# Loading x's third block second, x's rows in order of use, and block 3's spare rows from SyncE's queue

## The chip, the cores and the metric

The kernel runs on one core of a Trainium2 chip. The metric is the device time of one execution in microseconds, as the median of several runs. Besides these there is one execution with the hardware profiler on; all rows of a profile or a trace come from that one.

## What is computed

x has 2048 tokens of 448 features. The result mixes an attention branch and an MLP branch with one gate per token:

```python
x = A_x
g = _sigmoid((x * gate_w).sum(-1, keepdims=True))
a = _A_ref(x, A_wq, A_wk, A_wv, A_wo)       # 16 heads of 28, one shared key and value head
b = _B_ref(x, B_w1, B_w2, B_w3, B_w4)
return g * a + (1 - g) * b
```

The part that this change touches is the first half of the MLP branch:

```python
h = _gelu(_layernorm(x, axis=-1) @ w1)
# quarters of h's features are shifted by +1, -1, +2, -2 tokens: hs = concat(g0, g1, g2, g3) @ w2
x1 = x + hs
return x1 + _gelu(_layernorm(x1, axis=-1) @ w3) @ w4
```

## The kernel before, in words

The tokens are worked in four blocks of 512, numbered 0 to 3; a block has four tiles of 128 tokens. A float32 product is made of two or three products of rounded parts: an operand is split into a high and a low part (`split_x`, `split_w_chunk`, `h_part`), by a copy that rounds (ScalarE, mostly) and a subtraction (VectorE or GpSimd). The order of the instructions on each engine is that of the code.

The stages before the long MLP and attention loops, which is where the change is made:

- **Loads.** x comes in twice. `load_x(b)` (L284) brings block b transposed from `in_xT_dram` (1024 KB, tiles `xkv_b`), for the queries and for w1; `load_x1(b)` (L293) brings the same tokens as rows (896 KB, from `in_x_dram` into `x1`), for the layernorm's statistics and the residual. Nearly all loads are issued by SyncE (SP); a transfer of SyncE's queue is issued once the one before it has been, and once what it waits for has come.
- **Queries.** `first_queries` and `stage_q(u)` multiply the blocks of x by wq. `q_out(u)` (L327) copies a result out of PSUM on ScalarE and stores it to DRAM (`qd`), from ScalarE's queue but for u = 3 and the last, which SyncE stores.
- **Centring w1.** The layernorm's mean is taken out of w1 instead of out of x. `centre_w1` (L384) sums the columns of w1's transpose on VectorE (L388), writes the sums to DRAM in four small transfers (`cd`, L393) and reads them back to all partitions (`mean`, L395). `minus_mean` (L400) subtracts them on VectorE; then w1 is split (`split_w_high`, `split_w_low`: L113 to L116 on ScalarE, a memset of the upper half of its last chunk on GpSimd, L114, and L120 and L121 on VectorE).
- **w1 and gelu.** `stage_w1(b)` (L440) multiplies block b by w1 (L448 to L452), four tiles, each followed by a gelu on ScalarE (`hf`, L456), whose scale is the layernorm's 1/std (`rs_s`, from `ln1_tile`: L146 and L147 on VectorE, L150 and L151 on GpSimd), and a transpose on VectorE (`ht`, L457). The block is then written to DRAM by SyncE (`hd`, L462) and read back by `h_read(b)` (L467) in another layout, as `hraw`. There is one buffer of the tag `hraw`, so the next read waits until the block before has been split; xkv_3 uses it first.
- **Shift and w2.** `h_parts(b)` splits hraw into `hh` and `hl`, the operands of w2 (ScalarE L482, VectorE and GpSimd L483). hh and hl have 112 partitions of features and 16 spare ones, which `spare_h(b)` (L428) fills with the rest of the low part, by four small transfers inside the chip: from SyncE's queue for blocks 0 to 2, from ScalarE's for block 3. `stage_w2(b)` (L499) multiplies by w2 (L504, L505, L507) into one of two PSUM banks (`hs`), and VectorE adds a bank to x's rows (L509), which frees it.
- **Second layernorm, w3, w4.** Block 0 is normed, transposed through DRAM (`xd`, written at L174, read at L179 and L181 into `xr`) and split (`ln_split`, L673 and L676); `load_w34(i)` (L649, L650) loads the MLP's weights, which are split behind the tiles of the last w2 block (`weights`).

Buffers are taken from tags with a fixed number of them: `raw` has two (wqraw, xkv_0, then xkv_2, later ht and xt4), `hh` has two (w2raw, later hh of each block). All transfers share eight completion semaphores (DMAHW0 to DMAHW7 in the orders below), and an issue on a semaphore waits until the earlier transfer on it has landed.

Of the kernel before, what the change touches and what calls it, by code (L numbers as in the profile page):

```python
# [9 lines left out]
F32 = mybir.dt.float32  # L10
F32R = mybir.dt.float32r
# [6 lines left out]
P = 128  # L18
# [6 lines left out]
NB = S // 512  # L25
# [12 lines left out]
def f32(ap):  # L38
    return ap.bitcast(F32)
# [3 lines left out]
def gated_mix_kernel(  # L43
# [65 lines left out]
            nc.vector.tensor_tensor(wl[0:64, 3, :], raw[0:64, 3, :], f32(wh)[0:64, 3, :], ALU.subtract)  # L109
            nc.scalar.copy(wl[64:128, 3, :], raw[64:128, 3, :])  # L110

    def split_w_high(raw, wh, wl):
        nc.scalar.copy(wh[:, 0:3, :], raw[:, 0:3, :])  # L113
        nc.gpsimd.memset(f32(wh)[64:128, 3, :], 0.0)  # L114
        nc.scalar.copy(wh[0:64, 3, :], raw[0:64, 3, :])
        nc.scalar.copy(wl[64:128, 3, :], raw[64:128, 3, :])  # L116

# [147 lines left out]
    with tc.tile_pool(name="s1b", bufs=1) as s1b, \  # L265
# [10 lines left out]
        def h_tile(tag, name):  # L276
            return s1b.tile([P, 2112], F32R, tag=tag, bufs=2, name=name)[:, 0:2064].rearrange("p (m n) -> p m n", m=4)
# [6 lines left out]
        def load_x(b):  # L284
            if b == 1:
                xraw[b] = f32(s1b.tile([P, 4, 512], F32R, tag="w2x", bufs=1, name="xkv_1"))
            elif b == 3:
                xraw[b] = s1.tile([P, 4, 512], F32, tag="hraw", bufs=1, name="xkv_3")
            else:
                xraw[b] = s1.tile([P, 4, 512], F32, tag="raw", bufs=2, name=f"xkv_{b}")  # L290
            nc.sync.dma_start(xraw[b], xT[:, :, 512 * b:512 * b + 512])

        def load_x1(b):  # L293
            nc.sync.dma_start(x1[:, 4 * b:4 * b + 4, :],
                              x[512 * b:512 * b + 512, :].rearrange("(t p) d -> p t d", p=P))
# [11 lines left out]
        s1.tile([P, 16], F32, name="gap_w1")  # L307
        w1h = s1.tile([P, 4, D], F32R, name="w1h")
        w1l = s1.tile([P, 4, D], F32R, name="w1l")
        s1.tile([P, 48], F32, name="gap_x")  # L310
        w2h = s1b.tile([P, 4, D], F32R, name="w2h")
        w2l = s1b.tile([P, 4, D], F32R, name="w2l")
# [14 lines left out]
        def q_out(u, ps):  # L327
            b, g = divmod(u, NG)
            qf = s1.tile([P, 512], F32, tag="qf", bufs=4, name=f"qf_{u}")
            nc.scalar.copy(qf, ps)  # L330
            (nc.sync if u in (3, NU - 1) else nc.scalar).dma_start(qd[g, :, 512 * b:512 * b + 512], qf)

        def first_queries():
            ps = [mm1(f"q_{g}") for g in range(NG)]
# [49 lines left out]
        def centre_w1():  # L384
            cs = s1.tile([P, 32], F32, name="cs")
            nc.gpsimd.memset(cs, 0.0)
            for c in range(4):
                nc.vector.reduce_sum(cs[0:C, c:c + 1], w1t[0:C, c, :], axis=AX.X)  # L388
            ct = s1.tile([P, 32], F32, name="ct")
            nc.vector.transpose(ct, cs)  # L390
            cd = dram.tile([4, P], F32, name="cd")
            for p in range(4):
                nc.sync.dma_start(cd[:, 32 * p:32 * p + 32], ct[32 * p:32 * p + 4, :])  # L393
            mean = s1.tile([P, 4, P], F32, tag="hf", bufs=3, name="mean")
            nc.sync.dma_start(mean, cd.unsqueeze(0).broadcast_to([P, 4, P]))  # L395
            return mean[:, :, 0:C]

# [27 lines left out]
            o = min(c[0], 4 * 516 - 2 * step)  # L425
            return flat[:, o:o + 2 * step].rearrange("i (m n) -> i m n", m=2)[:, :, c[0] - o:c[0] - o + 512]

        def spare_h(b, queue):  # L428
            low = f32(hl[b])
            queue.dma_start(shifted(hh[b], 0, 2), low[0:32, 0, 1:513])  # L430
            queue.dma_start(shifted(hh[b], 2, 2), low[32:64, 0, 1:513])
            queue.dma_start(shifted(hl[b], 1, 2), low[64:96, 0, 1:513])
            queue.dma_start(shifted(hl[b], 3, 1), low[96:112, 0, 1:513])

        def low_w2(m):
            nc.vector.tensor_tensor(w2l[0:C, m, :], w2raw[0:C, m, :], f32(w2h)[0:C, m, :], ALU.subtract)
# [48 lines left out]
        def h_parts(b, m0, m1):  # L485
            if m0 == 0:
                h_begin(b)
            for m in range(m0, m1):
                h_part(b, m)
                if m == 0 and b < NB - 1:  # L490
                    spare_h(b, nc.sync)
            if m1 == 4:
                for tt in (hh, hl):
                    if b:
                        nc.gpsimd.tensor_copy(tt[b - 1][0:C, :, 514:516], f32(tt[b])[0:C, :, 2:4])
                    if b == NB - 1:
                        nc.gpsimd.memset(f32(tt[b])[0:C, :, 514:516], 0.0)
# [16 lines left out]
        s1b.tile([P, 16], F32, name="gap_hl")  # L514
        w1raw = f32(h_tile("hl", "w1raw"))[:, :, 0:D]
        w1t = f32(h_tile("hl", "w1t"))[:, :, 0:D]
        nc.sync.dma_start(w1t[0:C, :, :], w1T.rearrange("(q p) n -> p q n", p=C))
        nc.sync.dma_start(w1raw, w1)
        high_x(0, 1, 2)
# [4 lines left out]
        split_w_chunk(wqraw, wqh, wql, 3)  # L524
        split_w_chunk(wqraw, wqh, wql, 0)
        q0 = first_queries()
        load_x(2)
        split_x(1, 0, 2)
        split_x(1, 2, 4)
        for g in range(NG):  # L530
            q_out(g, q0[g])
        mean = centre_w1()
        load_x1(0)
        s1b.tile([P, 32], F32, name="gap_hh")
        w2raw = f32(h_tile("hh", "w2raw"))[:, :, 0:D]
        nc.sync.dma_start(w2raw[0:C, :, :], w2.rearrange("(q p) n -> p q n", p=C))
        s1b.tile([P, 16], F32, name="gap_w2")
        load_x(3)
        for b in range(1, NB):
            load_x1(b)  # L540
        split_x(2, 0, 2)
        split_x(2, 2, 4)
        split_x(0, 0, 1)
# [4 lines left out]
            ln1_tile(0, t)  # L548
        stage_q(6)
        stage_q(7)  # L550
        split_w_high(w1raw, w1h, w1l)
        split_w_low(w1raw, w1h, w1l)
        stage_q(8)
        for t in range(4):
# [124 lines left out]

        xraw2[0] = big("xr_0").rearrange("p (c n) -> p c n", c=4)  # L680
        xt_read(0, xraw2[0])
        spare_h(NB - 1, nc.scalar)
        load_w34(0, s2a)
        vT = s2a.tile([P, 512], F32, tag="xn", bufs=1, name="vT")
        nc.gpsimd.memset(vT, 0.0)
# [504 lines left out]
```

## Time and profile before

| What | Value |
|---|---|
| Median of 3 runs | 912.26 us (912.13 to 913.19) |
| The profiled execution | 913.44 us |
| its span, first to last instruction | 911.6 us |
| TensorE busy | 900.1 us of the span |
| ScalarE, VectorE, GpSimd busy | 629.2, 523.8, 72.0 us |
| TensorE's granted clock, mean | 0.997 |

The prediction quotes several views of this execution. The page has the busy times. The timeline gives instructions in order of time (start, duration, engine, line, operation, output<-input; in brackets the engine's idle time before it and what ended that). The chain of waits follows the work that ended last back from its end. A view of waits has engine, line, what was waited for, and us in all, times, longest. PE is TensorE, ACT ScalarE, DVE VectorE, POOL GpSimd, SPq SyncE's queue of issues; L456 is line 456 of the kernel. A `DMA` piece runs to the landing of the transfer.

### The profile page before, as it was taken

Reading aid. Unit: us, or ns where it says so; the run is one execution under the profiler, and the core shown is the slowest. Engines: PE = TensorE matmul, PEld = TensorE weight load, DVE = VectorE, ACT = ScalarE, POOL = GpSimd, SP = SyncE. Lnnn points to the kernel's source line nnn. Section 1 sums busy time; section 2 is a strip of 40 time slices with the busy share of each in tenths; the row PEclk is TensorE's granted clock in tenths of the full one; section 3 lists DMA queues with packets and bytes.
Section 4 is the critical chain, followed back from the end, with each engine's and each line's share of the span. In section 5 each row is a group of like instructions: output and inputs, shape, how many; then the busy total and the mean of one; then the engine's idle time right before and its main releaser. Section 6 shows DMA issues by size and latency. Waiting matters only on the chain.

```text
span 911.6 us, 24209 instructions
## 1 busy us (share of the span) xinstructions
PE 900.1 (99%) x10390; PEld 628.7 (69%) x10390; DVE 523.8 (57%) x978; ACT 629.2 (69%) x998; POOL 72.0 (8%) x109
## 2 busy tenths in 40 slices
PE   9998999999999999999999999999999999999997
PEld 6897888888888888875555555555555555555554
DVE  4484563831431531136766776776677766767664
ACT  4523254332131231269999999999999999999994
POOL 1022400510000520020000000000000000000000
PEclk9999999999999999999999999999999999999999
DMA  9867766030120020010000001000011000010001
GB/s 297 290 171 201 189 191 171 13 99 1 34 54 1 18 69 1 1 51 24 15 25 15 23 15 55 23 25 16 24 33 36 25 14 25 15 55 14 15 15 44
DMA packets 51146, 54.77 MB, mean 60 GB/s; under 512 B 11964, under 2 KB 38316, under 8 KB 50924
## 3 DMA queue, kind: packets, MB, share of 16 engines
q1 hardware_dynamic: 47980, 48.03, 18.5%
q10 hardware_dynamic: 3056, 5.16, 1.6%
q8 instruction: 82, 1.34, 0.6%
q14 instruction: 28, 0.23, 0.1%
HBM read 36.35 MB, written 15.33 MB: 57 GB/s over the span
## 4 chain that ended last, share of the span: by engine, by line
PE 86%; DMA 8%; DVE 2%; ACT 2%; SPq 0%; issue 0%; POOL 0%; ACTq 0%; DVEq 0%; POOLq 0%
PE bank L936 26%; PE bank L207 19%; PE bank L886 6%; PE acc L737 5%; PE acc L735 5%; PE acc L736 5%; PE g L139 4%; PE g L140 4%; PE g L138 4%; PE pair L207 3%; DMA xkv<-in_xT_dram 2%; DMA x<-in_x_dram 2%; PE g L141 1%; PE g L142 1%; DMA hd<-ht 1%; DMA hraw<-hd 1%
## 5 line engine op out<-in xcount | busy, mean ns | idle before, releaser
L260 ACT ACTIVATE p<-bank 128x512 f32<-128x512 f32 x514 | 266.3, 607 | 4.8 <-PE bank L207 1.5
L936 PE MATMUL bank<-p,vext 128*32 128x256 f32 x4064 | 247.6, 382 | 0.4
L936 PEld LDWEIGHTS bank<-p,vext 128*32 128x32 f32 x4064 | 117.6, 109 | 116.0 <-ACT p L260 52.8
L998 DVE COPY p<-pair 128x1024 f32<-128x1024 f32 x125 | 153.1, 1225 | 57.5 <-PE pair L207 45.0
L725 ACT ACTIVATE gh<-g 128x512 fp32r<-128x512 f32 x55 | 32.9, 598 | 181.1 <-PE g L142 181.1
L860 DVE TENSOR_TENSOR o<-o,bank 128x256 f32<-128x256 f32 x222 | 93.5, 421 | 80.3 <-PE bank L936 70.2
L260 ACT ACTIVATE p<-p 128x1024 f32<-128x1024 f32 x126 | 138.1, 1096 | 0.0
L260 ACT ACTIVATE p<-pair 128x1024 f32<-128x1024 f32 x129 | 136.7, 1059 | 0.0
L727 DVE TENSOR_TENSOR gl<-gf,gh 128x512 fp32r<-128x512 f32 x55 | 39.8, 725 | 161.4 <-ACT gf L726 161.4
L207 PE MATMUL bank<-qh,kh 32*128 32x512 f32 x514 | 114.7, 444 | 0.0
L207 PE MATMUL pair<-qh,kh 32*128 32x512 f32 x510 | 113.9, 443 | 0.0
L207 PE MATMUL bank<-qh,kl 32*128 32x512 f32 x514 | 101.6, 389 | 0.0
L207 PE MATMUL bank<-ql,kh 32*128 32x512 f32 x514 | 101.3, 390 | 0.0
L207 PE MATMUL pair<-qh,kl 32*128 32x512 f32 x510 | 101.0, 389 | 0.0
L207 PE MATMUL pair<-ql,kh 32*128 32x512 f32 x510 | 100.6, 389 | 0.0
L207 PEld LDWEIGHTS bank<-qh,kh 32*128 32x128 f32 x514 | 47.5, 181 | 60.3 <-issue 37.9
L737 PE MATMUL acc<-w4h,gl 128*128 128x448 f32 x220 | 80.7, 367 | 0.0
L735 PE MATMUL acc<-w4h,gh 128*128 128x448 f32 x220 | 80.1, 364 | 0.0
L736 PE MATMUL acc<-w4l,gh 128*128 128x448 f32 x220 | 79.8, 363 | 0.0
L886 PE MATMUL bank<-wof,on 128*32 128x224 f32 (+1 forms) x984 | 69.5, 357 | 0.0
L140 PE MATMUL g<-ah,w3l 128*128 128x512 f32 x168 | 65.4, 389 | 0.0
L138 PE MATMUL g<-ah,w3h 128*128 128x512 f32 x168 | 65.4, 389 | 0.0
(200 smaller groups left out, 1389.0 us busy)
## 6 DMA issues: line engine op xcount, KB each, us to landing
rb<-rd SPq DMA_DIRECT2D x15, 256.0 KB
qd<-qf ACTq DMA_DIRECT2D x14, 256.0 KB
x<-in_x_dram SPq DMA_DIRECT2D x4, 896.0 KB
hd<-ht SPq DMA_DIRECT2D x16, 224.0 KB
hraw<-hd SPq DMA_DIRECT2D x4, 896.0 KB
xd<-xt SPq DMA_DIRECT2D x16, 224.0 KB
w34raw<-in_w_dram SPq DMA_DIRECT2D x7, 512.0 KB
qr<-qd SPq DMA_DIRECT2D x64, 56.0 KB
```

The lines of the kernel that those rows point to most:

```text
L138: nc.tensor.matmul(ps, wh[:, c, :], ah[:, c, :], start=(c == 0), stop=False)
L140: nc.tensor.matmul(ps, wl[:, c, :], ah[:, c, :], start=False, stop=False)
L207: nc.tensor.matmul(ps[j], k[h, keys], q[h, :], start=(r == 0), stop=(r == 2), tile_position=(32 * j, 0))
L260: nc.scalar.activation(p[:, heads], p[:, heads] if source is None else source, AF.Exp, scale=SCALE)
L727: nc.vector.tensor_sub(gl, gf, f32(gh))
L735: nc.tensor.matmul(ps, gh[:, tok], w4h[i][:, k, :], start=(f == 0), stop=False)
L736: nc.tensor.matmul(ps, gh[:, tok], w4l[i][:, k, :], start=False, stop=False)
L737: nc.tensor.matmul(ps, gl[:, tok], w4h[i][:, k, :], start=False, stop=(f == stop))
L860: nc.vector.tensor_add(o, o, pv)
L886: nc.tensor.matmul(ps[32 * i:32 * i + 32, :], a[:, c:c + 32], w, start=start, stop=stop, tile_position=(0, 32 * i))
L936: nc.tensor.matmul(pv[32 * j:32 * j + 32, :], vext[:, kt, :], p_of[k][:, j, qs], start=(k == ks[0]), stop=(k == ks[-1]), tile_position=(0, ...
L998: nc.vector.tensor_copy(pa[:, both], pairs[0])
```

## The change

Five edits, all ahead of the long loops:

- xkv_2 is loaded right behind xkv_1, ahead of w1's transpose and w1. It takes a buffer of the tag `hh` (2112 elements a partition, of which it uses 2048) instead of one of `raw`, which came free only when wqraw had been split.
- Rows of x are loaded in the order of use: block 0 ahead of the mean's read-back, block 1 ahead of w2raw, block 2 ahead of xkv_3, block 3 behind it. Before, block 0 came behind the mean, and blocks 1 to 3 behind w2raw and xkv_3.
- Query 3's store goes from SyncE's queue to ScalarE's.
- The upper half of w1h's last chunk is set to zero where the tile is made, instead of where w1 is split.
- Block 3's spare rows go from ScalarE's queue to SyncE's, behind the reads of xr.

The core of the diff:

```diff
@@ split_w_high
-    def split_w_high(raw, wh, wl):
+    def split_w_high(raw, wh, wl, clear=True):
         nc.scalar.copy(wh[:, 0:3, :], raw[:, 0:3, :])
-        nc.gpsimd.memset(f32(wh)[64:128, 3, :], 0.0)
+        if clear:
+            nc.gpsimd.memset(f32(wh)[64:128, 3, :], 0.0)
@@ load_x
             else:
-                xraw[b] = s1.tile([P, 4, 512], F32, tag="raw", bufs=2, name=f"xkv_{b}")
+                xraw[b] = f32(s1b.tile([P, 2112], F32R, tag="hh", bufs=2, name="xkv_2"))[:, 0:2048].rearrange(
+                    "p (m n) -> p m n", m=4)
@@ where w1h is made
         w1l = s1.tile([P, 4, D], F32R, name="w1l")
+        nc.gpsimd.memset(f32(w1h)[64:128, 3, :], 0.0)
@@ q_out
-            (nc.sync if u in (3, NU - 1) else nc.scalar).dma_start(qd[g, :, 512 * b:512 * b + 512], qf)
+            (nc.sync if u == NU - 1 else nc.scalar).dma_start(qd[g, :, 512 * b:512 * b + 512], qf)
@@ centre_w1
             mean = s1.tile([P, 4, P], F32, tag="hf", bufs=3, name="mean")
+            load_x1(0)
             nc.sync.dma_start(mean, cd.unsqueeze(0).broadcast_to([P, 4, P]))
@@ spare_h
-        def spare_h(b, queue):
+        def spare_h(b):
             low = f32(hl[b])
-            queue.dma_start(shifted(hh[b], 0, 2), low[0:32, 0, 1:513])
...
+            nc.sync.dma_start(shifted(hh[b], 0, 2), low[0:32, 0, 1:513])
...
@@ the order of the first stages
+        s1b.tile([P, 32], F32, name="gap_hh")
+        load_x(2)
+        s1b.tile([P, 16], F32, name="gap_w2")
         nc.sync.dma_start(w1t[0:C, :, :], w1T.rearrange("(q p) n -> p q n", p=C))
         nc.sync.dma_start(w1raw, w1)
...
         q0 = first_queries()
-        load_x(2)
...
         mean = centre_w1()
-        load_x1(0)
-        s1b.tile([P, 32], F32, name="gap_hh")
+        load_x1(1)
         w2raw = f32(h_tile("hh", "w2raw"))[:, :, 0:D]
         nc.sync.dma_start(w2raw[0:C, :, :], w2.rearrange("(q p) n -> p q n", p=C))
-        s1b.tile([P, 16], F32, name="gap_w2")
+        load_x1(2)
         load_x(3)
-        for b in range(1, NB):
-            load_x1(b)
+        load_x1(3)
...
-        split_w_high(w1raw, w1h, w1l)
+        split_w_high(w1raw, w1h, w1l, False)
...
-        spare_h(NB - 1, nc.scalar)
+        spare_h(NB - 1)
```

What that does to the order of issues is seen best on SyncE. First its queue from the load of xkv_1 to the last load of rows, before (xkv_2 and xkv_3 are blocks 2 and 3 of x transposed, x1 the rows of x, w1t and w1raw the two forms of w1; in brackets what the issue waits for):

```order
L291 DMA xkv_1_136<-in_xT_dram 128x4x512 [waits DMAHW1_49]
L517 DMA w1t_140<-in_w1T_dram 112x4x448 [waits DMAHW2_49]
L518 DMA w1raw_139<-in_w1_dram 128x4x448 [waits DMAHW3_49]
L291 DMA xkv_2_201<-in_xT_dram 128x4x512 [waits DMAHW4_49,DMAHW6_49,DVE_49,PE_49]
L331 DMA qd_80<-qf_3_219 128x512 [waits DMAHW0_49,Activation_49]
L393 DMA cd_230<-ct_228 4x32 [waits DMAHW4_49]
L395 DMA mean_235<-cd_230 128x512 [waits DMAHW4_49,DMAHW3_49,DMAHW7_49,DMAHW2_49,DMAHW1_49]
L294 DMA x1_70<-in_x_dram 128x4x448 [waits DMAHW0_49]
L536 DMA w2raw_239<-in_w2_dram 112x4x448
L291 DMA xkv_3_242<-in_xT_dram 128x4x512
L294 DMA x1_70<-in_x_dram 128x4x448 [waits DMAHW7_49]
L294 DMA x1_70<-in_x_dram 128x4x448 [waits DMAHW2_49]
```

Of the four cd writes the last is shown; it waits for DMAHW4, which xkv_2 has too. Block 3's rows follow. The same queue now, from w1's second form on (xkv_2 and w1t stand ahead of it, behind xkv_1):

```order
L525 DMA w1raw_140<-in_w1_dram 128x4x448 [waits DMAHW4_49]
L396 DMA cd_233<-ct_231 4x32 [waits DMAHW3_49]
L296 DMA x1_70<-in_x_dram 128x4x448 [waits DMAHW4_49]
L399 DMA mean_238<-cd_233 128x512 [waits DMAHW6_49,DMAHW3_49,DMAHW7_49,DMAHW1_49,DMAHW0_49]
L296 DMA x1_70<-in_x_dram 128x4x448
L541 DMA w2raw_242<-in_w2_dram 112x4x448 [waits DMAHW2_49]
L296 DMA x1_70<-in_x_dram 128x4x448 [waits DMAHW5_49]
L293 DMA xkv_3_245<-in_xT_dram 128x4x512 [waits DMAHW7_49]
L296 DMA x1_70<-in_x_dram 128x4x448 [waits DMAHW2_49]
```

The four loads of x1 are blocks 0 to 3 in turn; block 0 stands ahead of the mean, block 1 right behind it. The last cd write shares no semaphore with xkv_2 any more.

On ScalarE, the stores of queries 2 and 3 and the copies of block 2, before:

```order
L330 COPY qf_2_216<-q_2_163 128x512 [waits PE_49]
L331 DMA qd_80<-qf_2_216 128x512 [waits Activation_49]
L330 COPY qf_3_219<-q_3_164 128x512 [waits PE_49]
L129 CAST ahk_2_247<-xkv_2_201 128x1024 [waits DMAHW4_49]
L129 CAST ahk_2_247<-xkv_2_201 128x1024
```

and now:

```order
L333 COPY qf_2_219<-q_2_168 128x512 [waits PE_49]
L334 DMA qd_80<-qf_2_219 128x512 [waits DMAHW2_49,Activation_49]
L333 COPY qf_3_222<-q_3_169 128x512 [waits PE_49]
L334 DMA qd_80<-qf_3_222 128x512 [waits DMAHW5_49,Activation_49]
L130 CAST ahk_2_248<-xkv_2_143 128x1024 x2
```

Query 3's store stands ahead of the copies of block 2, and waits for DMAHW5, the semaphore of query 0's store.

On SyncE at the end of these stages, where block 0 of the second layernorm is read back (xr) and the first weights of w3 and w4 are loaded (w34raw), before:

```order
L331 DMA qd_80<-qf_15_941 128x512
L179 DMA xr_0_1028<-xd_0_924 128x3x512
L181 DMA xr_0_1028<-xd_0_924 64x512 x2
L649 DMA w34raw_0_1040<-in_w3_dram 128x4x256
L650 DMA w34raw_0_1040<-in_w4_dram 128x2x448
```

and now:

```order
L334 DMA qd_80<-qf_15_941 128x512
L180 DMA xr_0_1028<-xd_0_924 128x3x512
L182 DMA xr_0_1028<-xd_0_924 64x512 x2
L434 DMA hh_3_996<-hl_3_997 16x2x512
L435 DMA hh_3_996<-hl_3_997 16x2x512
L436 DMA hl_3_997<-hl_3_997 16x2x512
L437 DMA hl_3_997<-hl_3_997 16x512
L653 DMA w34raw_0_1040<-in_w3_dram 128x4x256
```

The four transfers of block 3's spare rows stand between the reads of xr and the weights; they have left ScalarE's queue, where they stood behind the last copies of block 3.

More of the change, by code (lines that the diff above doesn't have):

```diff
@@ L426, in shifted @@
             return flat[:, o:o + 2 * step].rearrange("i (m n) -> i m n", m=2)[:, :, c[0] - o:c[0] - o + 512]
-        def spare_h(b, queue):
+        def spare_h(b):
             low = f32(hl[b])
-            queue.dma_start(shifted(hh[b], 0, 2), low[0:32, 0, 1:513])
-            queue.dma_start(shifted(hh[b], 2, 2), low[32:64, 0, 1:513])
-            queue.dma_start(shifted(hl[b], 1, 2), low[64:96, 0, 1:513])
-            queue.dma_start(shifted(hl[b], 3, 1), low[96:112, 0, 1:513])
+            nc.sync.dma_start(shifted(hh[b], 0, 2), low[0:32, 0, 1:513])
+            nc.sync.dma_start(shifted(hh[b], 2, 2), low[32:64, 0, 1:513])
+            nc.sync.dma_start(shifted(hl[b], 1, 2), low[64:96, 0, 1:513])
+            nc.sync.dma_start(shifted(hl[b], 3, 1), low[96:112, 0, 1:513])
         def low_w2(m):
@@ L490, in h_parts @@
                 if m == 0 and b < NB - 1:
-                    spare_h(b, nc.sync)
+                    spare_h(b)
             if m1 == 4:
```

## The prediction

> **What bounds the kernel now.** First the engine line of the page, then TensorE's own waits (engine, line, what it waited for: us in all, times, longest).
>
> ```profile
> PE 900.1 (99%) x10390; PEld 628.7 (69%) x10390; DVE 523.8 (57%) x978; ACT 629.2 (69%) x998; POOL 72.0 (8%) x109
> ...
> PE hs L504 <- DVE x L509: 4.9, 2, 4.2
> ```
>
> TensorE is busy for 99% of the span, so only its few stalls can be won, and any new one is paid in full. Almost all of what it waits is one group: the product with w2 (L504) waits for VectorE to empty a PSUM bank (L509). TensorE's timeline shows the three places where it loses time before 130 us (start, duration, then in brackets the idle time and its cause).
>
> ```profile
> 37.26 0.36 PE L450 MATMUL h<-w1l,ahk 128*128 128x448 f32 x1
> ...
> 38.46 0.37 PE L450 MATMUL h<-w1l,ahk 128*128 128x448 f32 x1
> 38.99 0.47 PE L451 MATMUL h<-w1h,ahk 128*128 128x448 f32 x1 [0.16 <-POOL w1h L114]
> 39.30 0.36 PE L452 MATMUL h<-w1l,ahk 128*128 128x448 f32 x1
> ...
> 79.35 0.37 PE L505 MATMUL hs<-w2l,hh 112*128 112x448 f32 x1
> 79.56 0.36 PE L507 MATMUL hs<-w2x,hl 128*128 128x448 f32 x1
> 84.15 0.74 PE L504 MATMUL hs<-w2h,hh 128*128 128x448 f32 x1 [4.23 <-DVE x L509]
> ...
> 87.85 0.37 PE L507 MATMUL hs<-w2x,hl 128*128 128x448 f32 x1
> ...
> 122.41 0.37 PE L507 MATMUL hs<-w2x,hl 128*128 128x448 f32 x1
> 123.44 0.47 PE L504 MATMUL hs<-w2h,hh 128*128 128x448 f32 x1 [0.66 <-DVE x L509]
> 123.74 0.36 PE L505 MATMUL hs<-w2l,hh 112*128 112x448 f32 x1
> ```
>
> Undisturbed, products with w2 start 0.21 us apart (79.35 to 79.56), those with w1 0.20 us (37.26 to 38.46 are six steps). The big stall costs more than its 4.23 us, as this window shows (its last three columns are the granted clock, the DMA share and GB/s).
>
> ```profile
> 84.10:87.50 3.40, 3.35 (x9) 3.00 (x10) 2.13 (x5) 0.00 (x0) 0.68 (x3) 0.51 0.51 103
> ```
>
> After it the clock was 0.51 for 3.4 us. From 79.56 to 87.85 are eleven steps, 8.29 us where 11 x 0.21 = 2.31 were due: 5.98 lost. The second place, 122.41 to 123.74, is two steps: 1.33 - 0.42 = 0.91 lost, at full clock. The third, 38.46 to 39.30: 0.84 - 0.40 = 0.44 lost.
>
> Who sets the big stall is in the chain of waits, read back from it.
>
> ```profile
> 30.51 16.50 DMA x<-in_x_dram
> ...
> 57.97 4.52 DMA hd<-ht
> ...
> 62.62 0.30 SPq L467
> ...
> 74.06 6.55 DMA hraw<-hd
> ...
> 83.57 0.54 DVE x L509
> ```
>
> Block 1's rows of x are issued at 30.51 and need 16.50 us to land. VectorE's statistics on them stand ahead of block 0's last transposes, so h of block 0 is late written to DRAM (57.97) and read back (62.62); block 1's read waits for the work on block 0, whose buffer it takes (74.06, landing 80.61); and L509 stands behind block 1's split on VectorE: its end, 84.11, is 3.50 after that landing.
>
> **The change part by part.** *Rows of x in order.* VectorE's view:
>
> ```profile
> 37.96 0.61 DVE L121 TENSOR_TENSOR w1l<-w1raw,w1h 64x448 fp32r<-64x448 f32 x1
> 47.04 0.63 DVE L146 BATCH_NORM_STATS2 st_s<-x 128x6 f32<-128x448 f32 x1 [8.47 <-DMA x<-in_x_dram]
> ```
>
> VectorE idles 8.47 us for block 1's rows. In the new order they are issued right behind the mean, near 26.2 by the working below, with 896 KB and the mean ahead of them instead of 896 + 784 + 1024 KB and query stores. This stretch gives the speed:
>
> ```profile
> 32.00:48.00 16.00, 15.84 (x77) 13.96 (x76) 6.75 (x17) 8.36 (x14) 2.25 (x3) 1.00 1.05 389
> ```
>
> At 389 GB/s their 917,504 B take 2.36 us; behind a mean that lands at 31.7 (below) they are in near 34, ahead of 38.57, when VectorE is free for them. So the h chain starts up to 8.47 us earlier. It cannot keep all of it. Block 0's last parts stand behind the gelu of the last tile of block 2, which TensorE delivers with this matmul:
>
> ```profile
> 63.50 0.37 PE L452 MATMUL h<-w1l,ahk 128*128 128x448 f32 x1
> ```
>
> 63.87, and I allow 2.6 us for the gelu, the copies and GpSimd's subtraction behind it: block 1's read is issued near 66.5 instead of 74.06, lands at 66.5 + 6.55 = 73.1, and L509 ends at 73.1 + 3.5 = 76.6. TensorE asks for the bank at 79.77. The cover is 3.2 us; without it the stall comes back, up to the 5.98. I take the whole 5.98 as gone. What follows (blocks 2 and 3) is released by TensorE's own progress and moves with it.
>
> *Block 3's spare rows by SyncE.* The chain and SyncE's waits:
>
> ```profile
> 108.35 6.50 DMA hh<-hl
> ...
> 116.06 4.47 DMA w34raw<-in_w_dram
> ...
> SPq L181 <- DMA hh<-hl: 7.3, 1, 7.3
> ```
>
> SyncE holds back the last two reads of xr for 7.3 us, because their completion semaphores are those of the spare rows, and the first MLP weights stand behind them (116.06). Now the reads of xr go first, the spare rows behind them at about the same time as on ScalarE, the weights some 5 us earlier. The weights' split on VectorE is then done before the bank wait of 123.44: 0.91 gone. The spare rows themselves are needed here:
>
> ```profile
> 114.66 1.66 ACT L673 CAST ah<-xr 128x512 fp32r<-128x512 f32 x3 [5.60 <-DMA xr<-xd]
> ...
> 115.84 0.36 PE L504 MATMUL hs<-w2h,hh 128*128 128x448 f32 x1
> ```
>
> They landed at 114.85, 0.99 us before TensorE used them. Two reads of 128 KB now stand ahead of them: 256 KB at 389 GB/s are 0.67, which the 0.99 covers. Bounds: 0, and, if they are served only when the xr read that landed at 114.66 is in, 114.66 + 0.67 + 0.59 (their own 224 KB) = 115.92, or 0.1 late. I take 0. [...]
>
> *Zeros at once.* The 0.44 was GpSimd's memset of w1h, queued behind the first statistics. It now runs in the first 5 us: 0.44 gone.
>
> *Block 2 second; block 0's rows ahead of the mean.* This is where the change can lose. Four rows: block 1 of x in; w1T in (its first sum); SyncE's cd writes and its wait in them; the mean.
>
> ```profile
> 14.39 2.00 ACT L129 CAST ahk<-xkv 128x1024 fp32r<-128x1024 f32 x2 [2.16 <-DMA xkv<-in_xT_dram]
> ...
> 18.36 2.20 DVE L388 TENSOR_REDUCE cs<-w1t 112x1 f32<-112x448 f32 x4 [0.34 <-DMA w1t<-in_w1T_dram]
> ...
> 20.83 4.01 SPq L393 DMA_DIRECT2D cd<-ct  x4
> ...
> SPq L393 <- DMA xkv<-in_xT_dram: 2.8, 1, 2.8
> ...
> 25.84 4.65 DMA mean<-cd
> ```
>
> 1 MB of block 2 now stands ahead of w1T: 1,048,576 B / 389 GB/s = 2.70, so w1T is in at 21.06. The first cd write follows 20.83 - 18.36 = 2.47 later, at 23.53. The four took 4.01, of which 2.8 were a wait for block 2 on a shared semaphore; that wait goes, and they end at 23.53 + 1.2 = 24.7. The mean follows 1.0 later as now (24.84 to 25.84), at 25.7: what w1T loses, the wait gives back. But block 0's rows are issued at 24.7, on the same queue ahead of the mean: 917,504 B at 389 GB/s = 2.36, begun 1.0 earlier, so 1.36 more. The mean lands at 25.7 + 4.65 + 1.36 = 31.7 instead of 30.49. What that does is read from VectorE:
>
> ```profile
> 26.24 0.43 SPq L294 DMA_DIRECT2D x<-in_x_dram  x1
> ...
> 30.60 2.23 DVE L400 SCALAR_TENSOR_TENSOR w1raw<-mean,w1raw 128x448 f32<-128x448 f32 x4 [1.64 <-DMA mean<-cd]
> 33.44 0.63 DVE L146 BATCH_NORM_STATS2 st_s<-x 128x6 f32<-128x448 f32 x1 [0.61 <-DMA x<-in_x_dram]
> ```
>
> From the mean to the end of w1l VectorE has no pause but 0.61 for block 0's rows, which now come first. Without it w1l ends at 38.57 - 0.61 = 37.96; TensorE, without the memset's 0.44, uses its last piece at 38.86. So the mean may be 0.90 late, until 31.39; 31.7 costs 0.3 to 0.4, I take 0.4. Bounds of the landing: 30.4, if both transfers overlap fully (0 us), and, if the mean moves only when block 0's rows are in, 24.7 + (33.44 - 26.24) + 4.65 = 36.6, a stall of 5.2. Queue order with the issue latency overlapped is nearest, hence 31.7. [...]
>
> *Query 3's store on ScalarE.* It waits there for query 0's store, and the copies of block 2, now at 24.61, are queued behind it, with TensorE's products of block 2 behind them.
>
> ```profile
> 16.90 0.34 ACTq L331 DMA_DIRECT2D qd<-qf  x1
> ...
> 24.61 2.52 ACT L129 CAST ahk<-xkv 128x1024 fp32r<-128x1024 f32 x3 [4.76 <-DMA xkv<-in_xT_dram]
> 27.03 0.58 ACT L330 COPY qf<-q 128x512 f32<-128x512 f32 x1
> ...
> 104.52 3.03 DMA qd<-qf
> ```
>
> Query 0's store is issued at 16.90. Landing like the one at 104.52 (3.03), the copies start near 20; landing only when query 4 reuses its buffer without a wait (27.03), they start 2.4 us late. Block 2 itself is there by 14.39 + 2.70 = 17.1. They must start by 24.6, 7.7 us after the issue: I take 0, with 2.4 as the other end.
>
> **Sum.** -5.98 - 0.91 - 0.44 + 0.4 = -6.93, against the profiled execution (913.44, of which 911.6 is the span): 906.5, span 904.7. The runs' median is 912.26, so I forecast 912.26 - 6.93 = 905.3. A measurement here tells about 0.2% (1.8 us) from no change.
>
> **The rivals.** *A, the mean is late.* For: it shares its queue with 896 KB that were behind it. Half way between 31.7 and the far end 36.6 is 34.2: a stall of 2.8 instead of 0.4, 907.7. Rows show no clock loss after 0.66 us of idling and a loss after 4.23; between them I count none. *B, the h chain keeps a wait.* For: DRAM legs of 4.5 to 6.6 us that other loads can lengthen, with 3.2 us of cover. Half of the 5.98 returns: 908.3; all of it 911.3. *D, the late bank wait stays*, or the spare rows take its place: + 0.9, 906.2. *N, the change does not bring the rows earlier*, since issues wait on shared semaphores: 912. Against: block 1's load has no wait of its own in the new order. *C, slower.* The mean waits as block 1's rows did, 16.50 us in a full queue, instead of 4.65: 25.7 + 16.5 = 42.2, a stall of 42.2 - 31.4 = 10.8 and, as after the 4.23, 5.98 - 4.23 = 1.75 of slow clock: 912.26 - 7.33 + 12.55 = 917.5. It decides from where the stall and its slow clock pass 7.33 + 1.8, a mean later than about 38.8. Against: little else is queued at 25.
>
> **How the numbers follow.** Forecast 0.52, A 0.20, B 0.10, D 0.07, N 0.04, C 0.07. Range 904.6 to 908.6: from the stall of 0.4 gone and a little of the runs' spread, to A and the better half of B; it holds 0.52, 0.18 of A, 0.05 of B and D, 0.82. Faster by over 0.2%: the forecast, A, D and nearly all of B, 0.88; within: N and the rest of B, 0.05; slower: C, 0.07.
>
> **What would show it.** Right: no TensorE wait above 1 us before 130; the statistics of block 1 start near 39; block 1's h lands before 76; the first w1l product late by under 1 us; the weights issued near 105. Wrong: a TensorE gap near 37 above 1 us (A, C), or one at the third w2 tile (B, N), or one near 109 or 116 at the start of the last w2 block (D).

## The result, and the profile after

| | before | after | difference |
|---|---|---|---|
| median of 7 runs each, one chip | 912.13 us (909.90 to 913.19) | 906.18 us (905.26 to 909.25) | -5.95 |
| the profiled execution | 913.44 us | 905.92 us | -7.52 |
| its first product with w1 | 36.85 | 36.79 | -0.06 |
| its first product with w2 | 75.28 | 75.24 | -0.04 |
| its first product with w3 | 125.79 | 118.78 | -7.01 |

The ratio of the times is 0.9942, with a 95% interval of 0.9927 to 0.9957 (an estimate over all runs; the quotient of the two medians is 0.9935). The forecast was 905.3. Of the 7.52 us between the two profiled executions, 6.97 lie between the first w2 and the first w3 product, where the prediction put its two large terms, and next to nothing ahead of them.

TensorE's waits in the profile after (engine, line, what was waited for: us in all, times, longest; lines are up to 7 further down than before: L504 is now L508, L509 is L513 and L146 is L147):

```profile
PE h L452 <- ACT qf L333: 1.2, 1, 1.2
PE warm_ps L96 <- PEq L1182: 0.8, 1, 0.8
PE h L454 <- DVE w1l L121: 0.3, 1, 0.3
```

Both bank waits of w2 are gone. In their place stand two waits at the start of w1, of 1.17 us at its first product and 0.29 at its third. The window of the old big stall (busy time of PE, PEld, DVE, ACT and POOL, then granted clock, DMA share, GB/s), in the profile after:

```profile
75.00:91.00 16.00, 16.00 (x76) 14.16 (x76) 10.29 (x20) 6.08 (x11) 6.79 (x11) 1.00 0.72 203
```

TensorE is busy throughout, at clock 1.00. VectorE in the timeline after shows why:

```profile
20.04 2.20 DVE L391 TENSOR_REDUCE cs<-w1t 112x1 f32<-112x448 f32 x4 [3.48 <-DMA w1t<-in_w1T_dram]
...
32.03 2.23 DVE L404 SCALAR_TENSOR_TENSOR w1raw<-mean,w1raw 128x448 f32<-128x448 f32 x4 [4.97 <-DMA mean<-cd]
...
37.12 1.66 DVE L121 TENSOR_TENSOR w1l<-w1raw,w1h 128x448 fp32r<-128x448 f32 x3
...
39.24 0.61 DVE L147 BATCH_NORM_STATS2 st_s<-x 128x6 f32<-128x448 f32 x1
...
78.14 0.61 DVE L513 TENSOR_TENSOR x<-x,hs 128x448 f32<-128x448 f32 x1
```

Block 1's statistics start at 39.24 with no wait (47.04 before), and the bank is free at 78.14 + 0.61 = 78.75 (84.11 before). SyncE's queue of issues in the profile after:

```profile
22.51 1.30 SPq L396 DMA_DIRECT2D cd<-ct  x4
23.86 0.42 SPq L296 DMA_DIRECT2D x<-in_x_dram  x1
25.45 0.35 SPq L399 DMA_DIRECT2D mean<-cd  x1
25.84 0.43 SPq L296 DMA_DIRECT2D x<-in_x_dram  x1
...
69.38 0.31 SPq L471 DMA_DIRECT2D hraw<-hd  x1
...
106.04 0.61 SPq L653 DMA_DIRECT2D w34raw<-in_w_dram  x1
```

The four small writes take 1.30 instead of 4.01, block 1's rows are issued at 25.84 instead of 30.51, block 1's h is read back at 69.38 instead of 74.06, and the first MLP weights are issued at 106.04 instead of 116.06.

### The profile page after: what moved, and what is told of

Same layout as the page of the kernel before. It is cut to its first block, busy times and chain, and to the rows that moved or that the text cites. A ratio compares the mean times of both kernels' runs of the same rounds, so it can differ in the third digit from the quotient of the medians.

```text
span 904.1 us, 24210 instructions
## 1 busy us (share of the span) xinstructions
PE 896.7 (99%) x10390; PEld 627.6 (69%) x10390; DVE 524.8 (58%) x978; ACT 629.4 (70%) x998; POOL 72.2 (8%) x109
## 4 chain that ended last, share of the span: by engine, by line
PE 94%; DMA 3%; ACT 1%; DVE 1%; SPq 0%; issue 0%; ACTq 0%; DVEq 0%
PE bank L940 26%; PE bank L208 20%; PE bank L890 6%; PE acc L741 5%; PE acc L739 5%; PE acc L740 5%; PE g L141 4%; PE g L140 4%; PE g L139 4%; PE pair L208 2%; DMA w1t<-in_w1T_dram 1%; PE hs L509 1%; PE hs L508 1%; ACT p L261 1%; PE g L142 1%; PE g L143 1%
## 5 line engine op out<-in xcount | busy, mean ns | idle before, releaser
L140 PE MATMUL g<-al,w3h 128*128 128x512 f32 x168 | 65.4, 389 | 0.0
```

Source lines behind the costliest of these rows:

```text
L140: nc.tensor.matmul(ps, wh[:, c, :], al[:, c, :], start=False, stop=False)
```

## The experiments

Theory: the order of x's rows carries the big term, the spare rows the small one, and the rest cancels. Rivals: block 2's early load carries it; or the early stages have a gain that something eats. The kernels ran in three groups of four, each group on one chip together with runs of the kernel before:

| kernel | median, us (runs) | ratio to before (95%) | first w1 product | first w3 product |
|---|---|---|---|---|
| rows_only | 905.57 (6) | 0.9924 (0.9905 to 0.9943) | 35.82 | 118.45 |
| rows_undone | 908.59 (9) | 0.9948 (0.9932 to 0.9964) | 37.88 | 121.38 |
| spare_only | 912.60 (12) | 0.9994 (0.9981 to 1.0007) | 36.39 | 125.17 |
| spare_undone | 907.42 (6) | 0.9940 (0.9920 to 0.9960) | 37.48 | 119.47 |
| mean_first | 907.91 (7) | 0.9940 (0.9918 to 0.9962) | 35.66 | 119.62 |
| both_early | 909.54 (12) | 0.9966 (0.9953 to 0.9980) | 39.34 | 120.62 |
| block2_undone | 905.94 (7) | 0.9922 (0.9901 to 0.9944) | 39.04 | 122.58 |
| chain_first | 905.81 (6) | 0.9924 (0.9903 to 0.9945) | 35.55 | 116.83 |
| after_again | 906.95 (12) | 0.9945 (0.9928 to 0.9962) | 37.14 | 121.06 |
| zeros_undone | 906.62 (11) | 0.9943 (0.9922 to 0.9964) | 36.32 | 118.54 |
| mean_chain | 906.60 (7) | 0.9935 (0.9910 to 0.9959) | 36.75 | 119.79 |
| rows_chain | 906.24 (8) | 0.9934 (0.9911 to 0.9956) | 35.53 | 117.43 |

The last two columns are of the one traced execution of each. The median of before was 913.52, 912.60 and 912.07 in the three groups (in the table's order). An interval reaches 1.2 to 2.2 us to each side, so differences below that are read from traces here, not from medians. One figure of the traces is free of what happens ahead of w2: the time from the first product with w2 to the first with w3. It is 50.51 us before and 43.54 in the changed kernel.

**The rows' order alone (rows_only).** The kernel before, with the loads of block 1's and 2's rows moved ahead; block 0's stays behind the mean:

```diff
         mean = centre_w1()
         load_x1(0)
+        load_x1(1)
         ... w2raw
-        load_x(3)
-        for b in range(1, NB):
-            load_x1(b)
+        load_x1(2)
+        load_x(3)
+        load_x1(3)
```

> The kernel before with one part of the change alone: block 1's rows of x are issued right behind block 0's (which stay behind the mean), block 2's behind w2, block 3's last. Theory (the order of x's rows carries the gain): block 1's rows are in by 38.6, VectorE's 8.47 us of idling and TensorE's 4.23 with its slow clock go; the late bank wait (0.66) and the memset (0.16) stay: 6.0 us less than before, about 906.1. Rival (block 2's early load carries it, by clearing SyncE's queue and the shared semaphores): less than 2 us, 910 or more, with a TensorE wait above 2 us at the third w2 tile. Rival (no part is enough alone: w2's and x's third and fourth loads, now later, take the gain back with a new wait): a wait of TensorE at another line between 36 and 75 us.

It gives the whole gain. VectorE and then TensorE in the timeline of rows_only:

```profile
38.08 0.61 DVE L146 BATCH_NORM_STATS2 st_s<-x 128x6 f32<-128x448 f32 x1
...
77.08 0.61 DVE L509 TENSOR_TENSOR x<-x,hs 128x448 f32<-128x448 f32 x1
```

```profile
36.61 0.47 PE L450 MATMUL h<-w1l,ahk 128*128 128x448 f32 x1 [0.21 <-DVE w1l L120]
...
38.57 0.48 PE L451 MATMUL h<-w1h,ahk 128*128 128x448 f32 x1 [0.28 <-POOL w1h L114]
```

Block 1's statistics start at 38.08, the bank is free at 77.69, and from the first w2 to the first w3 product it needs 43.82 us. These two are TensorE's largest waits behind its first instruction; the second is the memset. The late bank wait is gone as well, where the expectation had it staying.

**The rows' order undone (rows_undone).** The changed kernel with the old order of blocks 1 to 3:

```diff
-        load_x1(1)
         ... w2raw
-        load_x1(2)
         load_x(3)
-        load_x1(3)
+        for b in range(1, NB):
+            load_x1(b)
```

> The changed kernel with block 1's, 2's and 3's rows of x back behind w2 and x's fourth block (block 0's rows stay ahead of the mean, block 2 of x stays second). Theory: block 1's rows wait behind 784 + 1024 KB, VectorE idles about 8 us for them, TensorE's 4.2 us wait with its slow clock is back: 6 us more than the changed kernel, about 912. Rival (block 2's early load carries the gain): at most 2 us more, 908 or less. In between (both share it: block 2's 1024 KB are out of the queue by then, so block 1's rows land near 43 instead of 47): about 909.

It came out near the third answer: 908.59, a ratio of 0.9948 where the order alone has 0.9924. That interval overlaps those of rows_only and of the changed kernel, so the median alone does not show a loss. SyncE's issue of block 1's rows and VectorE in the timeline of rows_undone, and TensorE at the third w2 tile:

```profile
28.35 0.68 SPq L296 DMA_DIRECT2D x<-in_x_dram  x1
...
43.09 0.63 DVE L147 BATCH_NORM_STATS2 st_s<-x 128x6 f32<-128x448 f32 x1 [2.70 <-DMA x<-in_x_dram]
...
81.26 0.61 DVE L513 TENSOR_TENSOR x<-x,hs 128x448 f32<-128x448 f32 x1
```

```profile
82.35 0.37 PE L508 MATMUL hs<-w2h,hh 128*128 128x448 f32 x1
```

Block 1's statistics start 3.9 us later than in the changed kernel, but 4.0 earlier than before: the rows are issued at 28.35 instead of 30.51 and need 14.7 us instead of 16.5. Which of the other edits does that, no run separates. The bank is free at 81.87, and TensorE asks at 82.35, so it does not wait; but it asks that late because it had lost 2.6 us itself by the first w2 product (77.86 against 75.24). So the rows' order is enough for the gain. It is not the only way to it: without it the other edits together keep the big stall away in this trace, with 0.48 us to spare.

**The spare rows alone, and undone (spare_only, spare_undone).** One line each, in the kernel before and, the other way round, in the changed one:

```diff
-        spare_h(NB - 1, nc.scalar)
+        spare_h(NB - 1, nc.sync)
```

> The kernel before with block 3's spare rows issued by SyncE, behind the reads of xr. Theory: the MLP's first weights are issued some 5 us earlier or more (SyncE's 7.3 us wait is gone), the late bank wait of 0.66 us goes, the big stall of 4.23 stays: 0.9 us less than before, 911.2. Rival (the spare rows now land behind xr and TensorE waits for them at the start of the last w2 block): no gain or up to 1 us more, 912 to 913. Rival (what TensorE waited for there was something else): no change, 912.1, with the 0.66 still there.

> The changed kernel with block 3's spare rows back on ScalarE's queue. Theory: SyncE's wait of about 7 us and TensorE's late bank wait of 0.66 are back: 0.9 us more than the changed kernel, 907.1. Rival (the shift of the semaphores by the other parts already removed that wait): the same as the changed kernel, 906.2, with no wait of SyncE above 1 us.

Alone it removes the late bank wait and leaves the big one, as this view of TensorE's waits in spare_only shows, but its time is that of before (0.9994), where 0.9990 was expected: too little to tell. In the trace, the time from the first w2 to the first w3 product is 49.72 us, 0.79 less than before.

```profile
PE hs L504 <- DVE x L509: 4.3, 1, 4.3
```

Undone, SyncE's wait returns (from the waits of SyncE's queue, spare_undone), yet no late bank wait:

```profile
SPq L182 <- DMA hh<-hl: 5.9, 1, 5.9
```

So the step "spare rows by SyncE: 0.91 gone" is right by itself and not needed beside the rows' order: either of the two edits removes that wait. Its margin is small with the order alone. It shows again as 0.30 (TensorE, rows_chain below, spare rows on ScalarE):

```profile
115.07 0.47 PE L506 MATMUL hs<-w2h,hh 128*128 128x448 f32 x1 [0.30 <-DVE x L511]
```

**Where the early stages lose (mean_first, block2_undone, both_early, chain_first).** ScalarE in the timeline of the changed kernel, between the mean and TensorE's 1.17 us wait:

```profile
12.92 2.00 ACT L130 CAST ahk<-xkv 128x1024 fp32r<-128x1024 f32 x2 [0.79 <-DMA xkv<-in_xT_dram]
...
33.76 1.32 ACT L113 CAST w1h<-w1raw 128x1344 fp32r<-128x1344 f32 x1 [4.84 <-DVE w1raw L404]
...
36.15 0.58 ACT L333 COPY qf<-q 128x512 f32<-128x512 f32 x1
```

TensorE's last query product, in its timeline after and then before:

```profile
35.23 0.39 PE L143 MATMUL q<-ahk,wql 128*128 128x512 f32 x1
```

```profile
36.62 0.39 PE L142 MATMUL q<-ahk,wql 128*128 128x512 f32 x1
```

It came 1.39 us earlier than before: block 1 of x was in by 12.92 instead of 14.39, and a wait of 0.32 us went. That is not shown to be the change's doing: rows_chain below, whose loads up to there are those of before, has 12.54 for block 1 and 35.30 for this product. Earlier or not, the first h product needs the PSUM bank of query 8, whose copy stands on ScalarE behind the rounding of w1, which waits for the mean. Four kernels move the links of that chain:

```diff
 mean_first, in centre_w1 and behind it
-            load_x1(0)
             nc.sync.dma_start(mean, ...)
+        load_x1(0)
 block2_undone: load_x(2) in the tag raw, behind first_queries again; query 3's store on SyncE
 both_early
-        load_x(2)
         nc.sync.dma_start(w1t ...)
         nc.sync.dma_start(w1raw, w1)
+        load_x(2)
+        load_x1(0)        (and no longer in centre_w1)
 chain_first
         minus_mean(mean)
-        for t in range(4):
-            ln1_tile(0, t)
         stage_q(6)
         stage_q(7)
+        stage_q(8)
         split_w_high(w1raw, w1h, w1l, False)
         split_w_low(w1raw, w1h, w1l)
-        stage_q(8)
+        for t in range(4):
+            ln1_tile(0, t)
```

> The changed kernel with the mean issued ahead of block 0's rows of x instead of behind them. Theory (the 896 KB ahead of it make the mean late, and the w1 chain behind it is what eats the time won by block 2 and the zeros): the mean lands 4.65 us after its issue, near 30.1 instead of 31.9; the wait of 1.17 us at the first w1 product goes; of the 0.29 at the third, up to 0.5 stays since VectorE now waits for block 0's rows: 1 us less than the changed kernel, 905.2. Rival (the mean is late because w1T is, and its queue does not matter): 906.2, with the wait of 1.2 still there.

The mean was subtracted from 30.81 instead of 32.03, and the 1.17 went. But block 0's rows came late, and their statistics stand ahead of w1's low part on VectorE; its timeline and TensorE's, mean_first:

```profile
30.81 2.23 DVE L403 SCALAR_TENSOR_TENSOR w1raw<-mean,w1raw 128x448 f32<-128x448 f32 x4 [3.04 <-DMA mean<-cd]
...
35.04 0.63 DVE L147 BATCH_NORM_STATS2 st_s<-x 128x6 f32<-128x448 f32 x1 [2.00 <-DMA x<-in_x_dram]
...
37.99 1.66 DVE L121 TENSOR_TENSOR w1l<-w1raw,w1h 128x448 fp32r<-128x448 f32 x3
```

```profile
38.63 0.47 PE L453 MATMUL h<-w1l,ahk 128*128 128x448 f32 x1 [2.39 <-DVE w1l L121]
```

A wait of 2.39 took the place of 1.17 + 0.29. The 0.5 expected for it was too small: block 0's rows, behind the mean, were not in before 35.04. The time is 907.91, not the 905.2 expected.

> The changed kernel with block 2 of x back at its old place and in its old buffer (issued once the first weights are split), and query 3's store back on SyncE; all else as changed. Theory (block 2 second wins nothing by itself: what the four small writes no longer wait, w1T is later): the mean lands within 1 us of the changed kernel's, time 905.5 to 906.5. Rival (block 2 second is part of the gain): 907.5 or more, with the mean 2 us or more later. Rival (block 2 second costs): 905 or less.

Median 905.94, as the theory has it: no gain of block 2's early load is to be seen beside the other edits. The traced execution is its longest (909.87). In it the mean is subtracted from 34.27, 2.24 later than in the changed kernel, which was the rival's sign; so what block 2 does to the mean stays open. Why that execution is long is told at the end.

> The changed kernel with block 2 of x issued behind w1T and w1 instead of ahead of them, and block 0's rows right behind block 2 instead of behind the four small writes. Theory: w1T is in some 1.6 us earlier (sums from 18.4), the mean has nothing large ahead of it and lands near 28.5, and TensorE does not wait for w1 at all: 1.5 us less than the changed kernel, 904.7. Rival (another chain ends there too: block 2's copies, some 2.5 us later, or the third w2 tile, whose cover was 0.97 us): half of that or nothing, 905.5 to 906.2, with a new wait at a product of block 2 or at the third w2 tile.

Slower than the changed kernel (0.9966 against 0.9942, intervals that just touch), where 1.5 us less were expected. The mean was hardly earlier (subtracted from 31.36, since SyncE issued it only at 26.61), and block 2's copies came late by what the prediction had as the far end of a term, though the transfer at fault is another. ScalarE in the timeline of both_early:

```profile
26.72 0.34 ACTq L334 DMA_DIRECT2D qd<-qf  x1
27.10 2.51 ACT L130 CAST ahk<-xkv 128x1024 fp32r<-128x1024 f32 x3 [6.17 <-DMA x<-in_x_dram]
```

Query 3's store waits on ScalarE until block 0's rows have landed, an event it has no use for (6.17 us of ScalarE's idling in the row above); a completion semaphore shared with them, as in the orders above, would explain it, but is not shown. Block 2's copies behind it start at 27.10, and TensorE waits for them, in the timeline of both_early:

```profile
28.20 0.50 PE L139 MATMUL q<-ahk,wqh 128*128 128x512 f32 x1 [1.22 <-ACT ahk L130]
...
29.46 0.50 PE L140 MATMUL q<-alk,wqh 128*128 128x512 f32 x1 [0.76 <-DVE alk L133]
```

> The changed kernel, loads untouched, with the work between the mean and the first w1 product in order of need: ScalarE copies query 8 out of its PSUM bank before it rounds w1, and VectorE subtracts w1's low part before block 0's statistics. Theory (TensorE's waits of 1.17 and 0.29 us are the tail of the w1 chain, so 1.4 us are to be had there): 904.8, no wait above 0.3 us at 36. Rival (block 0's statistics, now 2.3 us later, make the first gelu late, and with it a PSUM bank or the third w2 tile): 906.2 or more, with a wait there.

The loads are those of the changed kernel, and TensorE waits nowhere behind its first instruction in its trace. VectorE, chain_first:

```profile
34.02 1.70 DVE L121 TENSOR_TENSOR w1l<-w1raw,w1h 128x448 fp32r<-128x448 f32 x3 [0.85 <-ACT w1h L113]
```

The first w1 product is at 35.55, the first w3 product 1.95 us earlier than in the changed kernel. (This execution also had w1T 1.55 us earlier, so not all of that is the new order.) The median, 905.81, is not clear of the changed kernel's, and 904.8 was expected.

**Once more, and the combinations (after_again, zeros_undone, mean_chain, rows_chain).** The changed kernel itself; the changed kernel with the memset back in `split_w_high`; the edits of mean_first and chain_first together; and the kernel before with the edits of rows_only and chain_first and the early memset:

```diff
 zeros_undone
-        nc.gpsimd.memset(f32(w1h)[64:128, 3, :], 0.0)      (ahead of the loads)
-        split_w_high(w1raw, w1h, w1l, False)
+        split_w_high(w1raw, w1h, w1l)
```

> The changed kernel itself once more, for more executions of it on one chip with those below and a second trace of it. Theory (its runs differ because w1T, which now has block 2 ahead of it, lands up to 2 us later in some executions, so that the w1 chain is late and TensorE waits 1 to 1.5 us at the first w1 product, and the clock falls to half behind that wait in some of them): runs between 905 and 909.5, median 906 to 907; where its trace has the sums of w1T start after 21, the first w1 product is after 37.3. Rival (the spread lies elsewhere, behind 130 us): the first w3 product near 118.8 in a run whose time is 907 or more.

TensorE in the timeline of after_again, and its window behind the wait:

```profile
37.14 0.47 PE L452 MATMUL h<-w1h,ahk 128*128 128x448 f32 x1 [1.56 <-ACT qf L333]
...
38.11 0.74 PE L454 MATMUL h<-w1l,ahk 128*128 128x448 f32 x1 [0.30 <-DVE w1l L121]
...
111.99 0.44 PE L508 MATMUL hs<-w2h,hh 128*128 128x448 f32 x1 [0.25 <-DMA hh<-hl]
```

```profile
38.00:41.40 3.40, 3.29 (x9) 2.94 (x10) 3.33 (x9) 2.10 (x5) 1.41 (x2) 0.50 1.05 325
```

This execution took 908.48. From the first w1 to the first w2 product it needs 39.91 us, the other trace 38.45: the clock was 0.50 for 3.4 us. The theory's cause was wrong: w1T's sums began at 20.28, only 0.24 later than in the other trace, and the first w1 product came 0.35 later; most of the 2.28 us by the first w3 product is the clock. The last row is the spare rows, 0.25 late; the prediction's far end for that was 0.1.

> The changed kernel with the memset of w1h back behind the first statistics on GpSimd. Theory (TensorE waits for the w1 chain at the same place, so the 0.44 us were not to be had): the same time as the changed kernel, within 0.3 us, its waits at 36 to 39 us differently shared out. Rival (the memset counts by itself, as forecast): 0.44 us more, which would show as a wait of 0.16 to 0.3 for GpSimd at the fourth chunk with the first w2 product that much later than its start of w1 plus 38.45.

No difference in the median, 906.62 against 906.95. In its trace the mean was in early (subtracted from 31.28), and then the memset does show, as the rival has it; a quarter of a microsecond is below what the medians can tell. TensorE in the timeline of zeros_undone:

```profile
38.98 0.47 PE L454 MATMUL h<-w1h,ahk 128*128 128x448 f32 x1 [0.26 <-POOL w1h L115]
```

> The changed kernel with both: the mean ahead of block 0's rows of x, and the chain behind it in order of need (query 8's copy ahead of w1's rounding, w1's low part ahead of block 0's statistics, which no longer hold it up when their rows are late). Theory: no wait at 36 in any execution and no slow clock behind it: median 904.3 to 905, highest run below 907. Rival (the late rows make the gelu of block 0 late, or the third w2 tile): 906 or more with a wait there.

The rival came: no wait at 36, but one at the third w2 tile, TensorE in the timeline of mean_chain:

```profile
80.63 0.47 PE L507 MATMUL hs<-w2h,hh 128*128 128x448 f32 x1 [1.02 <-DVE x L512]
```

> The kernel before with the rows of x in order, the early memset and the chain behind the mean in order of need; block 2's load, query 3's store, the mean and block 3's spare rows stay as before. Theory (block 2 second, block 0's rows ahead of the mean and the spare rows' queue win nothing): as fast as the changed kernel or faster, 904.5 to 905.5. Rival (block 2 second wins once the chain behind the mean is short: TensorE's wait of 0.3 at 16.75 stays without it): 0.3 to 1 us slower than the kernel that has the mean first and this chain.

906.24, where 904.5 to 905.5 was expected: as fast as the changed kernel, without its block 2, mean and spare rows parts. No version is faster than the changed kernel by more than the intervals: the ratios of rows_only, block2_undone and chain_first (0.9922 to 0.9924, against 0.9942 and 0.9945) point that way and do not show it.

## Why the prediction was right, step by step

- **The big stall, -5.98: right, with the mechanism named.** rows_only shows it: from the first w2 to the first w3 product it saves 6.69 us of the 6.89 that the two bank waits were put at. Its cover was mis-sized: 3.2 us forecast, 79.72 - 78.75 = 0.97 measured (TensorE's first product of the third tile is at 79.72). The term that failed is the 2.6 us allowed from the gelu of block 2's last tile to block 1's read: it was issued at 69.38, not 66.5. GpSimd does block 3's statistics first, and its subtraction behind them (timeline of GpSimd, after):

```profile
66.64 0.55 POOL L151 TENSOR_TENSOR rs_s<-mv_s,epst 128x4 f32<-128x4 f32 x1 [1.91 <-DVE mv_s L148]
67.28 1.01 POOL L152 TENSOR_TENSOR rs_s<-rs_s,powt 128x4 f32<-128x4 f32 x1
68.25 1.10 POOL L487 TENSOR_TENSOR hl<-hraw,hh 112x512 fp32r<-112x512 f32 x1
```

  The same two steps stood in the chain of waits before, where the allowance could have been read from:

```profile
71.95 1.01 POOL rs_s L151
72.96 1.08 POOL hl L483
74.06 6.55 DMA hraw<-hd
```

  That is why mean_chain, whose read of block 1 is issued 1.49 us later (70.87), has a wait there.
- **The late bank wait, -0.91: gone, and two edits each remove it.** It goes with the spare rows alone (spare_only), and also without them (rows_only, spare_undone). Rival D's second half, late spare rows, shows as 0.25 in one of the changed kernel's two traces and in none of the eight other traces that issue them from SyncE. That they stand behind xr in one queue is not shown as the cause (the chain of waits, after_again):

```profile
105.41 6.45 DMA hh<-hl
```

  From issue to landing they took 6.45 us there, and 6.50 on ScalarE's queue before, so this row does not show that SyncE's queue made them later.
- **The zeros, -0.44, and the late mean, +0.4: the sum right, the terms not.** The mean landed at 25.45 + 6.48 = 31.93, forecast 31.7 (the chain of waits, after):

```profile
25.45 6.48 DMA mean<-cd
```

  But TensorE came 1.39 us earlier, which no step had, and then waited 1.17 + 0.29, and the binding link was ScalarE's copy of query 8, not w1's low part as the prediction had it. What TensorE had won it waited away, so that the first w2 product moved by 0.04 us: what -0.44 + 0.4 gives, for other reasons. That this part of the sum came out is luck. The prediction's own list has a TensorE wait above 1 us near 37 as a sign of being wrong, of rivals A and C; the wait of 1.17 is that sign, though the mean was nowhere near A's 34.2. The signs of being right came too: block 1's statistics at 39.24, its h in by 75.29, the weights at 106.04.
- **Query 3's store, 0: right, with less room than forecast.** ScalarE was held until 22.34, 6.69 us after the issue of query 0's store where 3.03 was taken, and block 2's copies start at 22.71, still ahead of the 24.61 of before. both_early shows the price when the store is held longer.
- **905.3 against 906.18.** The difference of 0.88 is smaller than the interval (1.4 us to each side) and needs no cause. The sum -6.93 fits the traced executions (-7.52 in time, -7.01 to the first w3 product), but each kernel's executions differ. Of the changed kernel's 19 runs, 14 lie between 905.26 and 907.17 and five between 908.48 and 909.25, these at mean clocks of 0.997 to 0.998 (one short run, 905.69, has 0.998 too). The one of these five that was traced has the half clock behind the wait at w1: 3.4 us x 0.5 = 1.7. The prediction counted no clock loss for waits between 0.66 and 4.23 us; that term was put at nothing, and behind the 1.56 + 0.30 us of after_again it was 1.5. That it is the cause in the other four is argued from their clock, not traced. The kernel before varies the same way: five of its 63 runs beside the experiments have a mean clock of 0.999 or 1.000 and a median of 909.82, so the 1.75 of slow clock inside the 5.98 is probably not lost in every execution.

## What to carry to other kernels

Where one engine's idle time is the head of a chain to a stall 40 us later, give its load the place in the queue that its use asks for, and price the cover at the far end by walking every instruction ahead of the releasing one on each engine, GpSimd's included. Time gained in an early stage was waited away here, since the last link ahead of its consumer waited for something else (1.39 us gained at the last query product, 1.17 + 0.29 us waited at w1): look for the copy or the bank that stands behind that wait in the order of its engine, and reorder there (in chain_first that took the wait away; that it took time away is not shown). Test each edit of a bundle alone and undone: here a part of one of five edits, alone, gave the whole gain, and the rest without it gave much of it.

## What the runs showed of the hardware

A short wait of TensorE cost the clock in some executions and not in others. At the start of w1 the traces have: 1.17 + 0.29 us idle, clock 1.00 behind it (after); 1.37 + 0.30, 1.00 (spare_undone); 2.39, 1.00 (mean_first); 1.33 + 0.29, 0.50 for 3.4 us (rows_undone); 1.21 + 0.30, 0.51 (block2_undone); 1.56 + 0.30, 0.50 (after_again). One of the windows, of block2_undone:

```profile
40.60:44.00 3.40, 3.40 (x11) 3.05 (x10) 3.30 (x9) 2.55 (x6) 0.79 (x1) 0.51 1.05 386
```

Each of the three lost about 1.5 us by the first w2 product (39.91, 39.98 and 40.00 us from the first w1 product, against 38.45). The length of the wait does not order them: 1.21 us cost the clock and 2.39 did not. Where it lies does so in part, as the distances between the changes of the clock show. The clock falls to 0.50 once more behind TensorE's last product, at 910.20 in the profile before and at 904.97 in the one after; in this window of after_again the mean of 0.68 puts that at 904.94:

```profile
904.80:905.20 0.40, 0.00 (x0) 0.00 (x0) 0.00 (x0) 0.00 (x0) 0.00 (x0) 0.68 0.06 20
```

In the five traces that also have a slow stretch earlier (before, spare_only, rows_undone, block2_undone, after_again) that stretch lasts 3.41 us, and from its start to the last fall there are 826.02, 822.61 and three times 866.99 us: 242, 241 and 254 times 3.413. In a trace without an earlier slow stretch, stretches of 3.413 us counted back from the last fall are the author's estimate from these five. Three stretches counted so, of block2_undone, of after and of mean_first:

```profile
37.28:40.69 3.41, 1.91 (x8) 1.06 (x7) 3.31 (x9) 2.46 (x6) 1.08 (x2) 1.00 1.06 365
```

```profile
34.57:37.98 3.41, 1.94 (x8) 1.06 (x7) 3.27 (x10) 2.71 (x5) 0.61 (x2) 1.00 1.07 314
```

```profile
34.51:37.92 3.41, 1.73 (x8) 1.05 (x6) 2.74 (x8) 2.16 (x4) 0.00 (x0) 1.00 1.07 366
```

TensorE's idle time in a stretch is its length less the first busy time. The next stretch was slow behind 1.50 (block2_undone), 1.63 (rows_undone), 1.71 (after_again) and, for the big stall, 2.52 (spare_only) and 3.39 (before); it was not behind 1.37 (spare_undone), 1.45 (both_early) and 1.47 (after). But it was not slow either behind 1.68 in mean_first and 1.80 in spare_only, each the first part of a wait that runs on into the next stretch, so the idle time in one stretch does not order these cases alone.

The same load was in up to 3.03 us apart. In the eight traces that load w1T behind block 2, with the same queue up to there, VectorE waits for it and its sums start between 18.49 and 21.52. In the six that load it ahead they start between 16.21 and 19.16, but in four of these VectorE did not wait for it, so these times do not tell when it landed.
